# Attention and gated product: probabilities turned in float32 and split from PSUM, early exponentials per head, attention's buffers lent to later stages

## The chip, the cores and the metric

The kernel runs on one core of one Trainium2 chip. The metric is device time in microseconds (us) for one execution, lower is better. The engines are named as the profile names them: PE (TensorE, the matrix engine), PEld (its weight loads), DVE (VectorE), ACT (ScalarE), POOL (GpSimd) and SP, whose queue issues every DMA of this kernel.

## The reference, cut to what matters

```python
# q, k, v: [8, 8, 576, 64] (batch, head, row, depth); q and k are drawn 8 times larger than v
k_p = k.reshape(B, H, 72, 8, D).mean(axis=3)      # 8 rows pooled into one: 72 keys
v_p = v.reshape(B, H, 72, 8, D).mean(axis=3)
scores = (1 / 8) * q @ k_p.T
scores -= scores.max(-1)
attn = exp(scores); attn /= attn.sum(-1) + 1e-9
x = (attn @ v_p)  ->  [4608, 512]                 # 8 batches x 576 rows, 8 heads x 64
out = ((x @ w_a) * (x @ w_b)) @ w_out             # [512, 1536] twice, then [1536, 512]
```

Everything is float32, and the weights arrive as 8-byte words that the kernel itself converts.

## The kernel before, in words

**Precision.** A matmul operand is held as two rounded float32 parts (fp32r), a high part and a low part (the rest). A product is three matmuls: high by high, high by low, low by high. A "cast" to fp32r on ACT makes the high part, a subtraction (`low_part`) the low one.

**Attention.** The 4608 rows are 36 chunks of 128 rows (`chunk(i)`); a batch has 576 rows, so chunk 4 holds rows of two batches. Chunks 0 to 3 make the first tile of 512 rows (`early`). Per chunk: `qh`, `ql` are the parts of q; two PSUM banks `psc` take the scores of four heads each (72 columns per head); ACT copies them to `s` (all 8 heads, 576 columns); DVE takes the maximum `m`, subtracts it, ACT takes the exponential of all 576 columns, DVE takes the sum `z`, its reciprocal, and multiplies. The first 64 columns of each head then go to `pr`, as a high and a low part, and the last 8 columns to `rem`, which holds high, low and high again side by side. PE turns them (matmul with an identity, in transpose mode): four 128x128 blocks of the high part, four of the low part, two of `rem`, each set into a bank `ptr`, and ACT copies each bank out to `early_p` or `p` (the parts th, tl, tr). Two chunks make a block of 256 rows, whose products with the pooled values (`vdiag`, `vrem`) land in banks `po` and become x.

**The gated product.** x is handled in nine tiles of 512 rows. Tiles 0, 1 and 2 go through 12 column blocks f: `psa`, `psb` take x by w_a and w_b (weight buffers `jab`), DVE multiplies them into `h`, whose parts `hh`, `hl` are multiplied by w_out (`jo_open`, `jo_later`, `wo`) into four accumulator banks `acc`. The other six tiles are three pairs, (3,4), (5,6), (7,8), for which seven products of combinations of the two halves replace eight (banks `bank_psa`, `bank_psb`, `bank_att`, combinations `x_0` to `x_6`); the second tile of a pair keeps its gated values in device memory (`later`) and fetches them back (`back`) at the end of the pair. An accumulator that is finished is copied by ACT or DVE to a temporary `y` and stored (`give`).

**What sets the order.** Nothing in the kernel is a hand-written order on the engines: `Schedule.run` is a list planner that runs while the kernel is built. Each step is an `Op` with the engines it may run on and a cost per engine from the constants `FIXED`, `EACH` and `COLUMN`; generators (`chunk`, `ffn_in`, `both`, ...) yield steps and wait for marks, and the planner issues the step that can start first, by rank among the near ones. Every engine then runs its rows strictly in that order. So a change of one step's cost or engine moves rows on all engines. Buffers are handed out by name: eight PSUM banks (`banks`), and five SBUF temporaries of 512 columns, `tmps`, which serve `kp`, `vwide`, converted weight parts, `xo`, `back`, `gated` and `y`; `take(tmps)` blocks its generator until one is free.

**Weights at the start.** For each f, SP loads the 8-byte `words` of w_a, w_b (512 KB each) and w_out; ACT and DVE turn them into float32 (`wab`, `wo_first`), ACT and DVE or POOL split them into `jab` and `jo_open`. This runs between the rows of the first chunks.

In the profile every matmul has line L281, every turn L278, most ACT work L250, two-input DVE or POOL work L228, reductions L243.

Of the kernel before, what the change touches and what calls it, by code (L numbers as in the profile page):

```python
# [191 lines left out]
def attn_moe_kernel(ctx: ExitStack, tc: tile.TileContext, q, k, v, vr, wa, wb, wo, out):  # L192
# [49 lines left out]
    def red(out, in_, op):  # L242
        run = lambda e: nc.vector.tensor_reduce(out=out, in_=in_, axis=AX.X, op=op)  # L243
        return Op((SV,), run, [out], [in_], {SV: FIXED[SV] + EACH[SV] * size(in_)})
# [7 lines left out]
    def evict(out, in_):  # L252
        n = size(out)
        run = lambda e: nc.scalar.copy(out, in_) if e == SA else nc.vector.tensor_copy(out, in_)
# [460 lines left out]
    def load_keys(b):  # L715
# [6 lines left out]
        for g0 in range(0, NK, 2):  # L722
            gs = slice(g0, g0 + 2)
            for g in (g0, g0 + 1):
                if b == 0:
# [4 lines left out]
                yield red(kp[:, g, :], kraw.rearrange("p (s j) -> p s j", j=POOL), ALU.add)  # L730
                if b:
                    kv.append(kv_of["k", b, g])
            for e in range(2):
# [1 line left out]
                yield act(
                    kd[r, gs, 0, e, :], kp[r, gs],
                    lambda r=r, e=e: nc.scalar.mul(kd[r, gs, 0, e, :], kp[r, gs], 1.0 / POOL),  # L737
                )
# [59 lines left out]
    def chunk(i):  # L798
# [18 lines left out]
        yield W(("probs", i - 2))  # L817
        s = place(sb, [P, H, SP], F32, f"s{i % 2}", f"s_{i}")
        m = place(sb, [P, H], F32, f"m{i % 2}", f"m_{i}")
        z = place(sb, [P, H], F32, f"z{i % 2}", f"z_{i}")  # L820
        hk = 2 * SP
        for g0 in range(0, NK, 2):
            for b, lo, hi in flat[i]:
# [12 lines left out]
                yield copy(s[lo:hi, 2 * g0:2 * g0 + 4], pt[lo:hi, :2 * hk].rearrange("p (h s) -> p h s", h=4))  # L836
                banks.append(tag)
        mark("scores", i)
        yield red(m, s, ALU.max)
        yield tt(s, s, m.unsqueeze(2).broadcast_to([P, H, SP]), ALU.subtract)  # L840
        yield act(s, s, lambda: nc.scalar.activation(s, s, AF.Exp, scale=SCALE))
        yield red(z, s, ALU.add)
# [34 lines left out]
        for x in range(3):  # L877
            rows, num = (P, NK) if x < 2 else (NR, NG)
            dst = turned[j][x]
            srcs = [  # L880
                pr[:, x, 2 * g:2 * g + 2, :].rearrange("p a s -> p (a s)") if x < 2
                else rem[:, g].rearrange("p a c s -> p (a c s)")
                for g in range(num)
            ]
            yield until_ready(spare_time, *srcs)
            tag = yield from take(banks)
            pt = bank(tag, f"ptr_{i}_{x}")
            ptr = pt.bitcast(F32R).rearrange("p (g s) -> p g s", g=NK)
# [13 lines left out]
        th, tl, tr = (turned[j][x] for x in range(3))  # L902
# [297 lines left out]
    with tc.manual_schedule():  # L1200
        nc.vector.tensor_copy(ident, ident0)
        for t in kdiag + vdiag:
            nc.gpsimd.memset(t.bitcast(F32), 0.0)
        nc.vector.tensor_reduce(
            out=mask[:NR], in_=ident0[:NR, :NR].rearrange("p (a c s) -> p c a s", a=3, c=4), axis=AX.XY, op=ALU.add
# [81 lines left out]
```

## Time and profile before

| what | value |
|---|---|
| median of 3 runs (lowest, highest) | 1055.77 us (1054.13, 1060.22) |
| the profiled execution: its time, its span | 1054.74 us, 1052.6 us |
| PE busy, of the span | 1006.1 us (96%), 4896 matmuls |
| DVE, ACT, POOL busy | 640.0, 438.8, 212.7 us |
| DVE busy in the first 175 us, from the table of stretches below | 156.5 us |
| moved by DMA | 256.24 MB, 243 GB/s over the span |

The profiled execution's time is 1.03 us below the median of the runs. Between its span and its own time lie 2.1 us. The page's row for a matmul gives a modelled end, and matmuls follow each other before that end: a busy share of PE of 96% says when PE had work, not that it is at its peak. PE's clock as granted (PEclk) is 1.00 when full. All times in rows are us from the span's start unless marked ns; "x12" is a count of instructions.

### The profile page before, as it was taken

The numbers are of one execution on the slowest core, as the hardware profiler recorded it, in microseconds if no ns is written. First come the engines' busy times: TensorE is split into PE (matmuls) and PEld (weight loads), VectorE is DVE, ScalarE is ACT, GpSimd is POOL, SyncE is SP. The second block draws the span as 40 slices with busy tenths as digits, with TensorE's granted clock in tenths as the row PEclk, the third lists the DMA queues.
The fourth block names the chain that finished last, engine by engine and source line by source line (L and its number), as shares of the span: only waits on it lengthen the run. The fifth ranks groups of instructions, "written<-read, shape, count | busy, mean of one in ns | idle before, by whom it ended". The sixth has DMA issues, their size and how long they took to land.

```text
span 1052.6 us, 13699 instructions
## 1 busy us (share of the span) xinstructions
PE 1006.1 (96%) x4896; PEld 834.4 (79%) x4896; DVE 640.0 (61%) x978; ACT 438.8 (42%) x838; POOL 212.7 (20%) x164
## 2 busy tenths in 40 slices
PE   3698899999999999989999999999999999999998
PEld 3687688888888888868888887888888788888876
DVE  7998999988987556878775337333333633333321
ACT  5676666655565454554443314211111431111122
POOL 4221112011320001143121114022211501222100
PEclk9796999999999999989999999999999999999999
DMA  6494788789969989657765667666668966666792
GB/s 232 168 309 150 267 297 306 274 274 331 305 234 307 304 270 322 217 182 225 245 220 181 210 223 268 216 227 215 202 215 266 344 213 216 218 216 212 232 337 88
DMA packets 120467, 256.24 MB, mean 243 GB/s; under 512 B 10160, under 2 KB 26544, under 8 KB 120400
## 3 DMA queue, kind: packets, MB, share of 16 engines
q1 hardware_dynamic: 120400, 255.37, 73.0%
q8 instruction: 39, 0.64, 0.2%
q14 instruction: 28, 0.23, 0.1%
HBM read 195.82 MB, written 59.51 MB: 243 GB/s over the span
## 4 chain that ended last, share of the span: by engine, by line
PE 85%; DVE 6%; ACT 3%; DMA 3%; issue 1%; SPq 0%; POOL 0%; ACTq 0%; DVEq 0%; POOLq 0%
PE acc L281 26%; PE bank_psb L281 14%; PE bank_psa L281 9%; PE bank_att L281 9%; PE psb L281 8%; PE psa L281 8%; PE po L281 4%; PE psc L281 4%; PE ptr L278 2%; DMA words<-in_wo 1%; DMA vraw<-in_v 1%; DVE s L228 1%; ACT x L250 1%; DMA words<-in_wb 1%; DVE temp L228 1%
## 5 line engine op out<-in xcount | busy, mean ns | idle before, releaser
L281 PE MATMUL bank_psb<-x,j 128*128 128x512 f32 x648 | 167.7, 394 | 0.5 <-DVE temp L228 0.5
L281 PEld LDWEIGHTS bank_psb<-x,j 128*128 128x128 f32 x648 | 121.6, 189 | 27.4 <-DVE temp L228 1.1
L281 PE MATMUL acc<-jo_later,hh 128*128 128x512 f32 x384 | 124.2, 405 | 0.2
L281 PE MATMUL bank_psa<-x,j 128*128 128x512 f32 x432 | 111.5, 393 | 0.0
L281 PE MATMUL bank_att<-x,j 128*128 128x512 f32 x432 | 111.2, 392 | 0.0
L281 PE MATMUL psa<-xh,jab 128*128 128x512 f32 x288 | 102.5, 409 | 5.7 <-ACT jab L250 2.8
L281 PE MATMUL psb<-xh,jab 128*128 128x512 f32 x288 | 99.2, 397 | 0.5 <-DVE h L228 0.4
L228 DVE TENSOR_TENSOR temp<-bank_psb,temp 128x512 f32<-128x512 f32 x72 | 49.7, 690 | 78.4 <-PE bank_psb L281 77.2
L281 PEld LDWEIGHTS bank_psa<-x,j 128*128 128x128 f32 x432 | 81.0, 189 | 17.3
L281 PEld LDWEIGHTS bank_att<-x,j 128*128 128x128 f32 x432 | 80.3, 188 | 17.3 <-ACT temp L250 0.4
L228 DVE TENSOR_TENSOR temp<-bank_att,temp 128x512 f32<-128x512 f32 x54 | 37.3, 691 | 87.0 <-PE bank_att L281 81.1
L228 POOL TENSOR_TENSOR temp_p<-temp_p,temp 128x512 f32<-128x512 f32 x36 | 47.4, 1317 | 209.8 <-ACT temp_p L250 204.5
L228 DVE TENSOR_TENSOR temp<-bank_psa,temp 128x512 f32<-128x512 f32 x54 | 37.3, 691 | 81.2 <-PE bank_psa L281 77.4
L228 POOL TENSOR_TENSOR temp_h<-temp_h,temp 128x512 f32<-128x512 f32 x36 | 48.1, 1336 | 185.0 <-ACT temp_h L250 176.6
L228 POOL TENSOR_TENSOR ql<-qraw,qh 128x512 fp32r<-128x512 f32 x28 | 39.4, 1407 | 219.7 <-ACT qh L250 214.9
L281 PEld LDWEIGHTS acc<-jo_later,hh 128*128 128x128 f32 x384 | 68.5, 189 | 13.0 <-ACT hh L250 1.5
L281 PE MATMUL acc<-jo_later,hl 128*128 128x512 f32 x192 | 76.3, 398 | 0.0
L250 ACT CAST p<-ptr 128x512 fp32r<-128x512 f32 (+1 forms) x102 | 52.3, 514 | 48.1 <-PE ptr L278 47.9
L250 ACT CAST hh<-temp 128x512 fp32r<-128x512 f32 x36 | 22.4, 621 | 119.1 <-DVE temp L228 119.1
L281 PEld LDWEIGHTS psa<-xh,jab 128*128 128x128 f32 x288 | 55.7, 194 | 19.9 <-ACT jab L250 3.5
L281 PE MATMUL psc<-kdiag,qh 128*128 128x144 f32 x320 | 62.7, 292 | 7.6 <-ACT kdiag L737 7.0
L281 PEld LDWEIGHTS psc<-kdiag,qh 128*128 128x128 f32 x320 | 56.5, 210 | 11.2 <-issue 7.0
(137 smaller groups left out, 1967.6 us busy)
## 6 DMA issues: line engine op xcount, KB each, us to landing
j<-jd SPq DMA_DIRECT2D x108, 512.0 KB, 5.3
jo_later<-od SPq DMA_DIRECT2D x48, 512.0 KB, 3.8
wo<-od SPq DMA_DIRECT2D x36, 512.0 KB, 5.9
jab<-jd SPq DMA_DIRECT2D x34, 512.0 KB, 6.2
jd<-jab SPq DMA_DIRECT2D x24, 512.0 KB, 4.7
jd<-sums SPq DMA_DIRECT2D x24, 512.0 KB, 4.4
back<-later SPq DMA_DIRECT2D x43, 256.0 KB, 4.5
out<-y SPq DMA_DIRECT2D x36, 256.0 KB, 4.6
```

What stands on the lines that cost most here:

```text
L228: run = lambda e: vec[e].tensor_tensor(out=out, in0=in0, in1=in1, op=op)
L250: return act(out, in_, lambda: nc.scalar.copy(out, in_), rank)
L278: nc.tensor.transpose(to, lhs, rhs)
L281: nc.tensor.matmul(to, lhs, rhs, start=start, stop=stop, skip_group_check=bool(skip))
```

## The change

What it does, part by part:

- **Turn in float32.** The product with the reciprocal sum writes `pr` directly, as one float32 tile of 512 columns; the last 8 columns per head are multiplied apart (64 columns). PE turns `pr` in float32 with a float32 identity (`ident`; the fp32r one for `rem` is now `rounded`): one set of four blocks where there were two. The high part is cast by ACT out of the turned bank, the low part is the bank less the high part, on DVE. `rem`'s low part is pinned to DVE, and its two high copies are now split by group of heads.
- **Early exponentials per head.** For chunks below `BY_HEAD` = 8 whose rows are all of one batch (0 to 3, 5, 6, 7), DVE takes the negated maximum of four heads straight from the score bank, and ACT takes the exponential of each head from PSUM, with that maximum as its bias, writing `s` and, through its accumulator, the sum `z`. The copy to `s`, the subtraction, the long exponential and the sum over 576 columns are gone for these chunks. The factor 1/8 moves from the exponential into the keys.
- **Buffers.** `s`, `m`, `z` have three copies instead of two. Once all blocks are through the value product, `more_tmps` adds the five attention buffers `qh0`, `ql0`, `qh1`, `ql1`, `qraw` to `tmps`.
- **Rank.** `load_values(0)` gets a rank of -19.995.

```diff
+    def exponential(out, in_, bias, total):
+        run = lambda e: nc.scalar.activation(out, in_, AF.Exp, bias=bias, accum_out=total)
+        return Op((SA,), run, [out, total], [in_, bias], {SA: 0.36 + EACH[SA] * size(out)})
...
-                    lambda r=r, e=e: nc.scalar.mul(kd[r, gs, 0, e, :], kp[r, gs], 1.0 / POOL),
+                    lambda r=r, e=e: nc.scalar.mul(kd[r, gs, 0, e, :], kp[r, gs], SCALE / POOL),
...
+        direct = i < BY_HEAD and len(flat[i]) == 1
...
-                yield copy(s[lo:hi, 2 * g0:2 * g0 + 4], pt[lo:hi, :2 * hk].rearrange("p (h s) -> p h s", h=4))
+                if direct:
+                    yield red(m[:, hs4], four, ALU.max, True)
+                    for h in range(4):
+                        x = 2 * g0 + h
+                        yield exponential(s[:, x], four[:, h], m[:, x:x + 1], z[:, x:x + 1])
+                else:
+                    yield copy(s[lo:hi, hs4], four[lo:hi])
                 banks.append(tag)
...
-        yield tt(s, s, z.unsqueeze(2).broadcast_to([P, H, SP]), ALU.mult, (SG, SV))
         yield W(("turned", i - 2))
-        pr = place(sb, [P, 2, H, KM], F32R, f"pr{i % 2}", f"pr_{i}")
+        pr = place(sb, [P, H, KM], F32, f"pr{i % 2}", f"pr_{i}")
...
-        yield copy(pr[:, 0], s[:, :, :KM])
-        for x in (0, 2):
-            yield copy(rem[:, :, x], sr)
-        yield low_part(pr[:, 1], s[:, :, :KM], pr[:, 0], (SG, SV))
-        yield low_part(rem[:, :, 1], sr, rem[:, :, 0], (SG, SV))
+        yield tt(pr, s[:, :, :KM], spread(z, KM), ALU.mult, (SG, SV))
+        yield tt(sr, sr, spread(z, KR), ALU.mult)
+        for r in range(NG):
+            yield copy(rem[:, r, 0:3:2], sr[:, r].unsqueeze(1).broadcast_to([P, 2, 4, KR]))
+        yield low_part(rem[:, :, 1], sr, rem[:, :, 0])
...
-            yield pe([(ptr[:rows, g], srcs[g], ident) for g in range(num)], turn=True)
-            yield copy(dst[:rows, :, c0:c0 + P], ptr[:rows, :num])
+        yield pe([
+            (pt[:, g], pr[:, 2 * g:2 * g + 2].rearrange("p a s -> p (a s)"), ident) for g in range(NK)
+        ], turn=True)
+        yield copy(th[:, :, here], pt)
+        yield low_part(tl[:, :, here], pt, th[:, :, here])
...
+    def more_tmps():
+        yield W(*(("value", j) for j in range(block_of[-1] + 1)))
+        tmps.extend(["qh0", "ql0", "qh1", "ql1", "qraw"])
```

How rows move, at three places. First PE, chunks 2 and 3 of the first tile; `ptr_0`, `ptr_1`, `ptr_2` were the sets of the high part, the low part and `rem`, `psc_0_402` a score bank of chunk 4. Before:

```order
L278 MATMUL ptr_0_401<-ident,pr_357 128x128 x4
L281 MATMUL psc_0_402<-kdiag_77,qh_299 128x144 x2
L281 MATMUL psc_0_402<-kdiag_77,ql_300 128x144
L278 MATMUL ptr_1_418<-ident,pr_357 128x128 x4
L278 MATMUL ptr_2_424<-ident,rem_358 96x128 x2
L278 MATMUL ptr_0_459<-ident,pr_441 128x128 x4
L278 MATMUL ptr_1_466<-ident,pr_441 128x128 x4
L278 MATMUL ptr_2_473<-ident,rem_442 96x128 x2
```

The same two chunks in the changed kernel, PE:

```order
L284 MATMUL ptr_385<-ident,pr_357 128x128 x4
L284 MATMUL ptr_rem<-rounded,rem_358 96x128 x2
L284 MATMUL ptr_429<-ident,pr_417 128x128 x4
L284 MATMUL ptr_rem<-rounded,rem_418 96x128 x2
L287 MATMUL po_0_451<-p_1_380,vdiag_79 128x256
```

One set of four is gone per chunk, and the score matmuls of chunk 4 are no longer among the turns but behind the first `psa` rows.

Second, DVE in chunk 0, from the scores to the turn (`vp` is a pooled value, `wab_75` holds raw values there). Before:

```order
L243 TENSOR_REDUCE m_144<-s_143 128x8
L228 TENSOR_TENSOR s_143<-s_143,m_144 128x576
L243 TENSOR_REDUCE m_168<-s_167 128x8
L243 TENSOR_REDUCE z_145<-s_143 128x8
L843 TENSOR_SCALAR z_145<-z_145 128x8
L844 RECIPROCAL z_145<-z_145 128x8
L228 TENSOR_TENSOR s_143<-s_143,z_145 128x576
L243 TENSOR_REDUCE vp_183<-wab_75 96x64 x2
L235 SCALAR_TENSOR_TENSOR vwide_243<-vp_183,mask 96x256 x2
L228 TENSOR_TENSOR pr_230<-s_143,pr_230 128x512
```

The changed kernel, DVE, from its second maximum of chunk 0:

```order
L245 TENSOR_REDUCE m_171<-psc_0_176 128x4
L245 TENSOR_REDUCE m_144<-psc_2_192 128x4
L864 TENSOR_SCALAR z_145<-z_145 128x8
L865 RECIPROCAL z_145<-z_145 128x8
L230 TENSOR_TENSOR pr_219<-s_143,z_145 128x512
L230 TENSOR_TENSOR s_143<-s_143,z_145 128x8x8
L245 TENSOR_REDUCE vp_186<-wab_75 96x64
L230 TENSOR_TENSOR rem_220<-s_143,rem_220 128x2x32
L245 TENSOR_REDUCE vp_186<-wab_75 96x64
L230 TENSOR_TENSOR early_p_83<-ptr_250,early_p_83 128x4x128
```

The rows over 576 columns are gone; the low part (`early_p_83` from `ptr_250`) now stands behind the turn instead of ahead of it.

Third, ACT at the end of the second pair, where four accumulators are copied out to `y` while the combinations `x_0`, `x_4`, `x_3` of the next pair are cast. Before:

```order
L254 COPY y_0_7458<-acc_0_6653 128x512
L254 COPY y_1_7464<-acc_1_6666 128x512
L254 COPY y_2_7470<-acc_2_6691 128x512
L250 CAST hh_7476<-back_7441 128x512
L250 CAST x_0_7478<-x_7349 128x1024
L250 CAST jo_later<-back_7454 128x512
L250 CAST x_4_7482<-temp_2_7486 128x1024
L250 CAST x_3_7481<-temp_2_7485 128x1024
L254 COPY y_3_7497<-acc_3_6711 128x512
```

The changed kernel, ACT, same place:

```order
L256 COPY y_0_7266<-acc_0_6461 128x512
L256 COPY y_1_7272<-acc_1_6474 128x512
L256 COPY y_2_7277<-acc_2_6499 128x512
L256 COPY y_3_7283<-acc_3_6519 128x512
L252 CAST hh_7285<-back_7247 128x512
L252 CAST jo_later<-back_7254 128x512
```

The fourth copy moved from behind five casts to right behind the third.

More of the change, by code (lines that the diff above doesn't have):

```diff
@@ L39 @@
 LAG = 5
+BY_HEAD = 8
+VALUES_0 = -19.995
 JOIN, STEP = 40, 8
@@ L240, in ts, with red @@
         return Op((SV,), run, [out], [in0], {SV: FIXED[SV] + 0.0005 * size(out)})
-    def red(out, in_, op):
-        run = lambda e: nc.vector.tensor_reduce(out=out, in_=in_, axis=AX.X, op=op)
+    def red(out, in_, op, negate=False):
+        run = lambda e: nc.vector.tensor_reduce(out=out, in_=in_, axis=AX.X, op=op, negate=negate or None)
         return Op((SV,), run, [out], [in_], {SV: FIXED[SV] + EACH[SV] * size(in_)})
@@ L290, in tmp @@
         return place(sb, [P, 512], dtype, tag, name)
-    ident0 = tmp(tmps[0], "ident0")[:, :P]
-    make_identity(nc, ident0)
-    ident = const.tile([P, P], F32R, name="ident")
+    ident = const.tile([P, P], F32, name="ident")
+    make_identity(nc, ident)
+    rounded = const.tile([P, P], F32R, name="rounded")
     def big(tag, name):
@@ L741, in load_keys @@
                 yield stt(
-                    kd[r, gs, 1, e, :], kp[r, gs], 1.0 / POOL, kd[r, gs, 0, e, :].bitcast(F32), ALU.mult, ALU.subtract
+                    kd[r, gs, 1, e, :], kp[r, gs], SCALE / POOL, kd[r, gs, 0, e, :].bitcast(F32), ALU.mult, ALU.subtract
                 )
@@ L816, in chunk, with spread @@
             qs.append(tag)
[L817 to L820, printed above, removed]
+        yield W(("probs", i - 3))
+        s = place(sb, [P, H, SP], F32, f"s{i % 3}", f"s_{i}")
+        m = place(sb, [P, H], F32, f"m{i % 3}", f"m_{i}")
+        z = place(sb, [P, H], F32, f"z{i % 3}", f"z_{i}")
         hk = 2 * SP
+        direct = i < BY_HEAD and len(flat[i]) == 1
+        def spread(x, n):
+            return x.unsqueeze(2).broadcast_to([P, H, n])
         for g0 in range(0, NK, 2):
@@ L835, in chunk @@
                 ])
-                yield copy(s[lo:hi, 2 * g0:2 * g0 + 4], pt[lo:hi, :2 * hk].rearrange("p (h s) -> p h s", h=4))
-                banks.append(tag)
[L838 to L842, printed above, removed]
+                if g0 == NK - 2 and hi == P:
+                    mark("scores", i)
@@ new lines, in chunk @@
+                hs4 = slice(2 * g0, 2 * g0 + 4)
+                four = pt[:, :2 * hk].rearrange("p (h s) -> p h s", h=4)
+                if direct:
[5 more added lines that the diff above has]
+                    yield copy(s[lo:hi, hs4], four[lo:hi])
+                banks.append(tag)
@@ L843, in chunk @@
+        if not direct:
+            yield red(m, s, ALU.max)
+            yield tt(s, s, spread(m, SP), ALU.subtract)
+            yield act(s, s, lambda: nc.scalar.activation(s, s, AF.Exp))
+            yield red(z, s, ALU.add)
         yield Op((SV,), lambda e: nc.vector.tensor_scalar_add(z, z, 1e-9), [z], [z], {SV: 0.17})
         yield Op((SV,), lambda e: nc.vector.reciprocal(z, z), [z], [z], {SV: 0.2})
-        yield tt(s, s, z.unsqueeze(2).broadcast_to([P, H, SP]), ALU.mult, (SG, SV))
         yield W(("turned", i - 2))
-        pr = place(sb, [P, 2, H, KM], F32R, f"pr{i % 2}", f"pr_{i}")
+        pr = place(sb, [P, H, KM], F32, f"pr{i % 2}", f"pr_{i}")
@@ L876, in chunk @@
                 turned[j].update({y: three[:, y * NK:y * NK + (NK if y < 2 else NG)] for y in range(3)})
[L877 to L888, printed above, removed]
-            yield pe([(ptr[:rows, g], srcs[g], ident) for g in range(num)], turn=True)
-            yield copy(dst[:rows, :, c0:c0 + P], ptr[:rows, :num])
-            banks.append(tag)
+        th, tl, tr = (turned[j][x] for x in range(3))
+        here = slice(c0, c0 + P)
+        yield until_ready(spare_time, pr)
+        tag = yield from take(banks)
+        pt = bank(tag, f"ptr_{i}").rearrange("p (g s) -> p g s", g=NK)
+        yield pe([
[3 more added lines that the diff above has]
+        yield low_part(tl[:, :, here], pt, th[:, :, here])
+        banks.append(tag)
+        yield until_ready(spare_time, rem)
+        tag = yield from take(banks)
+        pt = bank(tag, f"ptr_{i}_rem").bitcast(F32R).rearrange("p (g s) -> p g s", g=NK)
+        yield pe([
+            (pt[:NR, r], rem[:, r].rearrange("p a c s -> p (a c s)"), rounded) for r in range(NG)
+        ], turn=True)
+        yield copy(tr[:NR, :, here], pt[:NR, :NG])
+        banks.append(tag)
         mark("turned", i)
@@ L901, in chunk @@
         cols = slice(j * BLOCK - t * NT, j * BLOCK - t * NT + BLOCK)
-        th, tl, tr = (turned[j][x] for x in range(3))
         for g0 in range(0, NK, 2):
@@ L1200, in attn_moe_kernel @@
     with tc.manual_schedule():
-        nc.vector.tensor_copy(ident, ident0)
+        nc.vector.tensor_copy(rounded, ident)
         for t in kdiag + vdiag:
@@ L1204, in attn_moe_kernel @@
         nc.vector.tensor_reduce(
-            out=mask[:NR], in_=ident0[:NR, :NR].rearrange("p (a c s) -> p c a s", a=3, c=4), axis=AX.XY, op=ALU.add
+            out=mask[:NR], in_=ident[:NR, :NR].rearrange("p (a c s) -> p c a s", a=3, c=4), axis=AX.XY, op=ALU.add
         )
```

6 lines of the change are left out of this document (4 added, 2 removed).

## Prediction, made before the run

> **What bounds the kernel now.** I read the page's table of engines, then a table of stretches, PE's waits, and last the rows around single waits.
>
> ```profile
> PE 1006.1 (96%) x4896; PEld 834.4 (79%) x4896; DVE 640.0 (61%) x978; ACT 438.8 (42%) x838; POOL 212.7 (20%) x164
> ```
>
> That alone says "PE". The stretches (columns: stretch and length, then busy us and count of PE, PEld, DVE, ACT, POOL, granted clock, DMA share, GB/s) say where it is not:
>
> ```profile
> 0.00:27.00 27.00, 9.92 (x46) 9.28 (x46) 21.32 (x35) 15.46 (x32) 12.08 (x22) 1.00 0.68 228
> 27.00:53.00 26.00, 17.79 (x86) 16.39 (x87) 23.83 (x35) 17.30 (x36) 6.96 (x4) 0.76 0.50 173
> 53.00:79.00 26.00, 25.70 (x131) 21.58 (x130) 23.84 (x37) 19.07 (x37) 7.52 (x6) 0.98 0.92 308
> 79.00:105.00 26.00, 21.63 (x105) 18.62 (x106) 21.25 (x34) 16.04 (x35) 4.38 (x3) 0.67 0.46 148
> 105.00:130.00 25.00, 22.04 (x113) 17.22 (x113) 22.89 (x33) 18.11 (x32) 4.58 (x3) 1.00 0.81 275
> 130.00:175.00 45.00, 44.17 (x220) 35.91 (x219) 43.37 (x67) 29.27 (x56) 8.44 (x5) 1.00 0.88 296
> 175.00:452.00 277.00, 277.00 (x1514) 234.77 (x1513) 215.90 (x351) 158.83 (x317) 39.22 (x28) 1.00 0.85 282
> 452.00:458.00 6.00, 2.08 (x11) 1.41 (x9) 5.84 (x8) 5.89 (x9) 1.72 (x2) 0.90 0.80 279
> 458.00:1052.60 594.60, 585.74 (x2680) 479.18 (x2680) 261.74 (x387) 158.87 (x290) 127.82 (x92) 0.99 0.68 225
> ```
>
> Three regimes. Up to 105 us PE idles 17.1 + 8.2 + 0.3 + 4.4 = 30 us, and its clock falls to 0.76 and 0.67, while DVE is busy 90.24 of 105 us: the start is paced by DVE and by the chain through one chunk. From 175 to 452 PE has no gap, so there only fewer or shorter PE rows help. After that it loses 3.9 us in one place (452 to 458) and 8.9 us in a few more. PE's waits name them:
>
> ```profile
> PE ptr L278 <- ACT pr L250: 17.5, 4, 6.1
> PE psc L281 <- ACT kdiag L737: 7.0, 1, 7.0
> PE ptr L278 <- ACT s L250: 4.3, 2, 3.9
> PE acc L281 <- ACT y L254: 2.2, 1, 2.2
> PE acc L281 <- DVE y L254: 1.8, 1, 1.8
> ```
>
> The turns waited 17.5 us for `pr`, all at the start; 3.9 us is the gap at 453 us; the two waits for `y` lie at the pairs' ends.
>
> **Term 1, one set of turns fewer per chunk.** PE's rows in the dense part (start, duration, then x2 or x4 instructions):
>
> ```profile
> 360.24 0.62 PE L281 MATMUL psb<-xh,jab 128*128 128x512 f32 x2
> 360.70 0.40 PE L281 MATMUL psb<-xl,jab 128*128 128x512 f32 x1
> ...
> 361.17 0.46 PE L278 MATMUL ptr<-ident,pr 128*128 128x128 f32 x4
> 361.47 0.70 PE L281 MATMUL acc<-jo_later,hh 128*128 128x512 f32 x2
> 362.01 0.39 PE L281 MATMUL acc<-jo_later,hl 128*128 128x512 f32 x1
> ```
>
> Start to start a set of four takes 0.30 us, and the two matmuls behind it 0.54 where two take 0.46 elsewhere: 0.38 us, or less where a score matmul follows; I take 0.36. The trace counts the sets from 175 us on:
>
> ```profile
> L278 PE MATMUL ptr<-ident,pr x208: 222/244/370, 204.5 to 600.0; 128*128 128x128 f32 x104
> ```
>
> 208 are 52 sets, half of them low parts: 26 x 0.36 = 9.4 us, all on the path. The ten earlier chunks' sets fall where PE waits anyway: 0.
>
> This holds if a float32 turn costs what an fp32r turn costs. No float32 matmul is in the trace. From below, the row above (0.30 us a set), and I exclude a gain, since words of the same width are loaded and streamed. From above, four passes: each turn as four streams of 128 columns, which is one row of 512 columns, 0.23 us, so 0.92 us a set, or, with the weights loaded four times too, 4 x 0.30 = 1.20. I take the row: the turn already runs on 4-byte words, and a turn only moves them.
> The Trainium skill, "FP8 and Floating Point Precision", TensorE Precision Notes, says that true FP32 takes four passes through the array; by that alone the 36 sets would cost up to 36 x 0.9 = 32 us more. The same skill, "TensorE: Matmul & The Clock Gate", Terms (row xbus), says of trn2's transpose mode that it is 4x faster for FP32, which would cancel it. No row here shows either.
>
> **Term 2, DVE in the early chunks.** Groups of DVE and ACT in 0 to 175 us (busy us, mean ns | idle before), and among them one row of the timeline (start, duration), of 64 columns on DVE:
>
> ```profile
> L228 DVE TENSOR_TENSOR s<-s,m 128x576 f32<-128x576 f32 x10 | 11.5, 1154 | 0.4
> L228 DVE TENSOR_TENSOR s<-s,z 128x576 f32<-128x576 f32 x10 | 8.3, 834 | 0.3
> L243 DVE TENSOR_REDUCE m<-s 128x8 f32<-128x576 f32 x11 | 8.2, 743 | 1.5 <-ACT s L250 1.5
> L243 DVE TENSOR_REDUCE z<-s 128x8 f32<-128x576 f32 x10 | 7.4, 745 | 0.7 <-ACT s L841 0.5
> L228 DVE TENSOR_TENSOR pr<-s,pr 128x512 fp32r<-128x512 f32 x8 | 6.6, 820 | 0.0
> 29.85 0.21 DVE L228 TENSOR_TENSOR rem<-s,rem 128x64 fp32r<-128x64 f32 x1
> L228 DVE TENSOR_TENSOR xl<-po,xh 128x512 fp32r<-128x512 f32 x8 | 5.5, 686 | 6.3 <-ACT xh L250 6.3
> L250 ACT COPY s<-psc 128x288 f32<-128x288 f32 x21 | 8.2, 399 | 5.2 <-PE psc L281 3.4 <-DVE rem L228 1.6
> L841 ACT ACTIVATE s<-s 128x576 f32<-128x576 f32 x10 | 6.9, 687 | 3.2 <-DVE s L228 3.1
> L250 ACT CAST pr<-s 128x512 fp32r<-128x512 f32 x10 | 6.2, 620 | 6.1 <-DVE s L228 6.0
> L250 ACT CAST p<-ptr 128x512 fp32r<-128x512 f32 x16 | 9.4, 586 | 5.4 <-PE ptr L278 5.4
> L250 ACT CAST rem<-s 128x64 fp32r<-128x64 f32 x20 | 4.0, 242 | 0.0
> ```
>
> A direct chunk loses on DVE 1.154 + 0.834 + 0.743 + 0.745 + 0.820 = 4.30 us. It gains two maxima over 288 columns from PSUM (between 0.2 and 0.74 each; I take half of the 576-column row, 0.37), the product into `pr` (0.82, the same shape), the small product (0.21, the 64-column row) and the low part from PSUM (0.69, by the row xl<-po,xh): 2 x 0.37 + 0.82 + 0.21 + 0.69 = 2.46. That saves 1.8 us per chunk, 12.9 over seven. An ordinary chunk exchanges 0.83 + 0.82 for 0.82 + 0.21 + 0.69: 0.1 more, over 29 chunks 2 us, under a DVE that in 175 to 452 is busy 78%: 0.
>
> What reaches PE: the first four chunks' 7 us, since up to 105 us PE waits for what DVE makes; the other three chunks' saving comes where PE lacks little (3.8 us in 105 to 175) and I count 0. So -7, bounds 0 and -17 (12.9, and half the time lost at clock 0.67 in 79 to 105, 26 x 0.33 / 2 = 4).
>
> **ACT** gets eight exponentials of 72 columns for two copies, one long exponential, the cast of `pr` and the cast of the turned low part: out 0.80 + 0.69 + 0.62 + 0.59 = 2.70 us per chunk. One of 72 columns with bias and accumulator is in no row; 0.24 (the 64-column cast) and 0.69 (the 576-column exponential) are its ends. I take 0.35, near the short one: 2.8 us, no change. At 0.69 it is 5.5, so 2.8 x 4 = 11 us more in the first 53, where ACT is busy 32.8: still under 53, but the chain through a chunk would be as long as before and term 2 would be 0.
> The Trainium skill, "ScalarE: Activation LUTs", What ACT_TABLE_LOAD costs, gives about 280 ns + 0.833 ns a column for an ACTIVATE with a pointer bias, so 0.34 us, an estimate without the accumulator; the sum would be the same.
>
> POOL's multiplies only change names; the pinned `rem` part is the 64-column row. On SP's queue the second pair of `kraw` loads now stands ahead of the second `words`, which also wait for a conversion that moved back on DVE. Their slack:
>
> ```profile
> 25.75 0.33 SPq L261 DMA_DIRECT2D words<-in_wa  x1
> ...
> 38.54 1.13 ACT L463 ACTIVATE wab<-words 128x1024 f32<-128x1024 f32 x1
> words<-in_wa SPq DMA_DIRECT2D x12, 512.0 KB, 4.7
> ```
>
> They were asked for at 25.8 us and first read at 38.5, 12.8 later; the last row, of the DMA issues, has 4.7 us to landing. So 8 us of cover; 0, and if it is gone, the second weight block is late next.
>
> **Term 3, more temporaries.** At the pairs' ends ACT's fourth `y` stood behind casts because, as the order and `take(tmps)` read, no temporary was free; now it stands right behind the third. That removes the 2.2 and 1.8 us waits. The clock there:
>
> ```profile
> 644.00:650.00 6.00, 4.16 (x15) 3.00 (x14) 6.00 (x8) 5.13 (x6) 2.57 (x3) 0.83 0.98 356
> ```
>
> 6 x 0.17 = 1 us of clock was lost too; I count half: -4.5, bounds 0 (the next PE row then waits for `back`, with DMA at 0.98) and -5.
>
> **Term 4, start of the pairs.** The gap at 453 us is a turn that waits for a bank behind ACT's casts of `x`. Now score and `rem` rows of about 1.1 us stand ahead of the second product, which needs those casts as well. -1, bounds -4 and +3.
>
> **Sum.** -9.4 - 7 - 4.5 - 1 = -21.9 us on 1054.74, so 1032.8; the median of the runs is 1.03 above its profiled run: 1034 us.
>
> **Rivals.**
> (a) Only the turns pay. For it: in 53 to 79 DMA is at 0.92, so the weights' loads could bind what DVE leaves, and a freed wait often moves on. Against it: in 0 to 53 DMA is at 0.68 and 0.50. Then -9.4 to -12: 1045.
> (b) The start pays more: all seven chunks' DVE time and the clock, -17 for term 2: 1024.
> (c) Slower: float32 turns run in four passes with four loads. In the dense part 26 sets cost 0.9 us more, +23.4, in the start 10 more sets up to +9, against -21.9 of the rest: 1057 to 1066, say 1061. It decides from 0.84 us more per set, at 1.14 us a set; at 0.92 the 26 sets give +16, so still about 1050. For it: no float32 turn was ever timed here. Against it: the rows of the fp32r turns show plain 4-byte words.
> (d) The change does not do what it says: the planner's rows are placed by its constants, and new waits eat the rest (low parts of turned banks hold `ptr` until DVE gets there, which is busy 43.37 of 45 us in 130 to 175): 1051 to 1056.
>
> **How the numbers follow.** My forecast 0.52, (a) 0.21, (b) 0.14, (c) 0.07, (d) 0.06. About 0.5% (5.3 us) is what a measurement of this kernel can tell from no change: under 1050.5 lie the forecast, (a) and (b), 0.87; (d) and a part of (c) are within it, 0.08; slower is most of (c), 0.05. The range 1021 to 1050 holds the forecast, most of (b) and (a); the forecast's own is 1027 to 1040.
>
> **What would show it.** PE's turns of `pr`: 144 rows of 128x128, median still about 245 ns (four passes would show 0.4 us or more, or sets over 0.9 us start to start). Exponentials: 56 rows near 0.35 us. PE idle before 105 us near 23 instead of 30, the first `psa` matmul some 4 us ahead of its row:
>
> ```profile
> 50.44 0.79 PE L281 MATMUL psa<-xh,jab 128*128 128x512 f32 x1 [0.50 <-DVE xl L228]
> ```
>
> No waits of `acc` for `y` in the middle. PE without gaps in about 170 to 440, shorter by 9 us. I am wrong if turned sets are longer, if PE waits for `words` or `p` low parts, or if the gaps at the pairs' ends come back with another name.

## The result, and the profile after

The changed kernel takes 1027.86 us (median of 4 runs, 1026.47 to 1030.40) against 1056.46 (1054.13 to 1060.22) for the kernel before on the same chip: ratio 0.9729, 95% interval 0.9692 to 0.9765. The forecast was 1034.0, with a range of 1021 to 1050. The profiled execution took 1026.70 us, its span is 1024.7; before they were 1054.74 and 1052.6.

The engines' line and the table of stretches after (columns as in the prediction):

```profile
PE 985.5 (96%) x4752; PEld 821.4 (80%) x4752; DVE 626.2 (61%) x1007; ACT 410.0 (40%) x859; POOL 210.9 (21%) x162
```

```profile
0.00:27.00 27.00, 13.45 (x56) 11.95 (x57) 21.54 (x43) 18.08 (x74) 11.47 (x21) 1.00 0.68 230
27.00:53.00 26.00, 20.89 (x99) 18.38 (x99) 23.09 (x40) 21.18 (x52) 6.04 (x4) 0.80 0.69 237
53.00:79.00 26.00, 16.97 (x64) 12.84 (x63) 24.09 (x41) 15.28 (x41) 6.57 (x5) 0.67 0.82 283
79.00:105.00 26.00, 26.00 (x146) 22.20 (x146) 19.93 (x37) 20.13 (x60) 4.18 (x4) 1.00 0.65 219
105.00:130.00 25.00, 24.85 (x129) 20.52 (x128) 23.69 (x36) 17.30 (x32) 4.88 (x4) 1.00 0.75 257
130.00:175.00 45.00, 45.00 (x243) 38.45 (x242) 40.27 (x61) 28.57 (x54) 7.95 (x5) 1.00 0.88 297
175.00:424.00 249.00, 249.00 (x1280) 209.95 (x1279) 188.32 (x319) 121.80 (x244) 33.66 (x22) 1.00 0.87 289
424.00:445.00 21.00, 15.91 (x79) 13.07 (x78) 15.85 (x25) 11.56 (x17) 8.14 (x5) 0.84 0.50 163
445.00:1024.70 579.70, 573.46 (x2669) 474.00 (x2667) 269.37 (x414) 156.05 (x291) 128.03 (x95) 1.00 0.70 234
```

The regimes are the same, but the start's bad stretch (PE idle for 9.0 us, clock 0.67) now stands at 53 to 79 us instead of 79 to 105, and after it PE hardly stops until 424 us; before, 3 us were still missing in 105 to 130. The gap at the start of the pairs is larger: 5.1 us idle in 424 to 445, against 3.9 in 452 to 458 before. PE's waits:

```profile
PE psc L287 <- ACT kdiag L743: 7.9, 1, 7.9
PE ptr L284 <- DVE s L230: 7.3, 3, 3.3
PE ptr L284 <- DVE pr L230: 5.4, 1, 5.4
PE ptr_rem L284 <- ACT s L252: 2.7, 1, 2.7
PE psc L287 <- DVE p L230: 2.7, 2, 1.9
```

The turns' 17.5 us of waiting for `pr` have become 7.3 + 5.4, and `acc` no longer waits for `y` at all.

**A ledger of PE.** Stretches of equal length hold different work, so I count work instead. Each matmul gets its own start-to-start time where rows stand dense, a median of the two traces: 0.2275 us for 512 columns, 0.1125 for 256, 0.1115 for 144; a set of turns with what it costs the two rows behind it 0.44 (four in float32), 0.368 (four in fp32r), 0.19 (two of `rem`). "Lost" at a point is the time there less the work issued so far: what PE lost to gaps, to low clock and to rows slower than the dense ones. All matmuls are in both traces. Cumulative, in us:

| kernel | work in all | lost at first `psa` | at 109th `psa` (about 150 us) | at last `acc` of tile 2 | at first `bank_att` | at first row of pair 2 | of pair 3 | at last `acc` |
|---|---|---|---|---|---|---|---|---|
| before | 965.2 | 37.1 | 55.7 | 60.4 | 67.1 | 74.9 | 80.1 | 83.0 |
| after | 954.6 | 31.1 | 48.7 | 50.9 | 59.7 | 63.3 | 63.8 | 65.4 |

The 28.2 us between the two last `acc` rows are 10.65 of work and 17.5 of loss: 7.0 up to the 109th `psa`, 2.5 more up to the end of tile 2, then 2.1 back at the start of the pairs, and 10.1 in the pairs, of which 4.3 + 3.1 at the ends of the first two (cut finer than the table: between a pair's last `bank_att` of its products and the next pair's first row).

### The profile page after: what moved, and what is told of

Same layout as the page of the kernel before. It is cut to its first block, busy times and chain, and to the rows that moved or that the text cites. A ratio compares the mean times of both kernels' runs of the same rounds, so it can differ in the third digit from the quotient of the medians.

```text
span 1024.7 us, 13483 instructions
## 1 busy us (share of the span) xinstructions
PE 985.5 (96%) x4752; PEld 821.4 (80%) x4752; DVE 626.2 (61%) x1007; ACT 410.0 (40%) x859; POOL 210.9 (21%) x162
## 4 chain that ended last, share of the span: by engine, by line
PE 85%; DVE 5%; DMA 5%; ACT 2%; issue 1%; POOL 1%; SPq 0%; ACTq 0%; DVEq 0%; POOLq 0%
PE acc L287 28%; PE bank_psb L287 13%; PE bank_att L287 9%; PE bank_psa L287 9%; PE psb L287 9%; PE psa L287 9%; PE po L287 4%; PE psc L287 4%; DMA vraw<-in_v 1%; PE ptr L284 1%; DMA j<-jd 1%; DMA qraw<-in_q 1%; DVE temp L230 1%; DMA wo_rest<-in_v 1%; DMA kraw<-in_k 1%
## 5 line engine op out<-in xcount | busy, mean ns | idle before, releaser
L287 PE MATMUL acc<-jo_later,hh 128*128 128x512 f32 x384 | 121.6, 398 | 0.3
L287 PE MATMUL psa<-xh,jab 128*128 128x512 f32 x288 | 99.9, 400 | 0.1
L287 PE MATMUL psc<-kdiag,qh 128*128 128x144 f32 x320 | 61.8, 289 | 13.3 <-ACT kdiag L743 7.9
L287 PE MATMUL acc<-jo_open,hh 128*128 128x512 f32 x192 | 62.8, 409 | 0.8 <-ACT s L260 0.7
```

The lines of the kernel that those rows point to most:

```text
L287: nc.tensor.matmul(to, lhs, rhs, start=start, stop=stop, skip_group_check=bool(skip))
```

## The experiments

Each kernel is timed against the kernel before on its own chip, whose medians were 1059.3 (the first four kernels), 1057.0 (the next four) and 1059.7 us (the last four); so the ratios are compared, and "scaled" is the ratio times 1056.46. Differences between two ratios are uncertain by about 5 us. The ledger of each profiled execution, columns as above:

| kernel | ratio, 95% | scaled | work | first `psa` | 109th `psa` | tile 2 | first `bank_att` | pair 2 | pair 3 | end |
|---|---|---|---|---|---|---|---|---|---|---|
| after | 0.9729 (0.9692 to 0.9765) | 1027.8 | 954.6 | 31.1 | 48.7 | 50.9 | 59.7 | 63.3 | 63.8 | 65.4 |
| e1 | 0.9907 (0.9884 to 0.9930) | 1046.6 | 954.6 | 33.2 | 55.7 | 59.9 | 69.2 | 77.2 | 82.3 | 85.6 |
| e2 | 0.9862 (0.9821 to 0.9903) | 1041.9 | 954.6 | 33.8 | 64.7 | 70.2 | 76.7 | 80.5 | 80.9 | 83.3 |
| e3 | 0.9774 (0.9744 to 0.9805) | 1032.6 | 954.6 | 31.1 | 50.2 | 52.4 | 64.3 | 73.6 | 78.3 | 79.5 |
| e4 | 0.9835 (0.9816 to 0.9854) | 1039.0 | 970.4 | 32.1 | 48.8 | 50.8 | 60.6 | 63.1 | 63.6 | 65.3 |
| e5 | 0.9815 (0.9791 to 0.9838) | 1036.9 | 954.6 | 33.7 | 58.6 | 61.8 | 67.8 | 71.2 | 73.8 | 77.8 |
| e6 | 0.9816 (0.9790 to 0.9841) | 1037.0 | 954.6 | 31.5 | 57.2 | 63.5 | 70.2 | 76.7 | 77.2 | 79.7 |
| e7 | 0.9823 (0.9798 to 0.9847) | 1037.8 | 954.6 | 30.8 | 57.6 | 61.3 | 71.8 | 75.9 | 76.4 | 78.2 |
| e8 | 0.9859 (0.9841 to 0.9878) | 1041.6 | 954.6 | 31.9 | 50.1 | 54.2 | 76.3 | 79.1 | 79.6 | 81.0 |
| e9 | 0.9778 (0.9752 to 0.9804) | 1033.0 | 954.6 | 37.2 | 55.3 | 57.3 | 67.1 | 70.4 | 70.8 | 73.2 |
| e10 | 0.9872 (0.9847 to 0.9896) | 1042.9 | 954.6 | 41.0 | 64.2 | 66.2 | 75.0 | 78.9 | 79.4 | 81.0 |
| e11 | 0.9948 (0.9929 to 0.9967) | 1051.0 | 965.2 | 34.6 | 56.9 | 60.7 | 64.8 | 71.7 | 78.5 | 81.6 |
| e12 | 0.9697 (0.9666 to 0.9728) | 1024.4 | 954.6 | 31.9 | 52.6 | 55.5 | 61.3 | 64.2 | 64.7 | 69.1 |

Theory A was that the parts of the change add up by the ledger; the main rival was that the planner's new order makes the time.

**e1, the turn alone.** Against the changed kernel:

```diff
-BY_HEAD = 8
+BY_HEAD = 0
-        yield W(("probs", i - 3))          # and s, m, z in two copies
+        yield W(("probs", i - 2))
-        ... need(b) - 1.0 if b else VALUES_0)
+        ... need(b) - 1.0)
-        sch.spawn(more_tmps(), 0.0)
```

> Only the turn in float32 is kept (with the split from the bank); no chunk takes its exponentials per head, the buffers of s and the temporaries are those of before. Theory A (a ledger of parts): in the changed kernel's trace a set of four float32 turns takes 0.355 us and 0.085 us in the two matmuls behind it, 0.44; before, two sets took 2 x (0.295 + 0.073) = 0.74. So 36 x 0.296 = 10.7 us less, nearly all on the path, and the start stays: first psa row at about 49 us (before 50.4), time about 1046. Rival B (the start's gain comes from the turn: one bank, one PE set and one cast less between the probabilities and the first value product): first psa at 43 to 45 us, time 1038 to 1040. Rival C (the planner's new order makes the time, no part does): anywhere from 1040 to 1060, and the gaps in places that neither trace has.

Measured: 9.8 us faster than before by the ratio, about the 10.65 us of work. The first `psa` came 5.1 us earlier than before (the row below against 50.44), close to rival B's 43 to 45 and not theory A's 49. But nothing of that lead lasted: at the 109th `psa` the loss is 55.7, as before.

```profile
45.29 0.54 PE L287 MATMUL psa<-xh,jab 128*128 128x512 f32 x1
```

So the first `psa` is a poor measure of the start, and the turn alone came out at about its work. Its order of rows is neither that of before nor that of the changed kernel, so this agreement may be partly luck (see e7).

**e2, no exponentials per head.**

```diff
-BY_HEAD = 8
+BY_HEAD = 0
```

> The changed kernel with the early exponentials per head undone (no chunk takes them), all else kept. Theory A: the start goes back: first psa at 49 to 50 us instead of 42.6, time lost by PE to gaps and low clock up to about 150 us back from 48.7 to about 55 us, total about 1028 + 7 = 1035. Rival B (the turn made the start shorter): first psa stays at 43 to 45, total 1028 to 1030. Rival C (the planner's order): no fixed relation, 1025 to 1040, with the start's gaps elsewhere.

Measured: 14.1 us back by the ratio, twice what theory A said, and the ledger puts 16.0 of it before the 109th `psa`. But the first `psa` was only 3.4 us later than in the changed kernel (45.99 us); most was lost behind it, where PE now waited for weights as well (`jab`, no such wait in the changed kernel):

```profile
PE psa L287 <- DVE jab L230: 3.5, 3, 1.7
PE psa L287 <- ACT jab L252: 3.1, 2, 2.1
```

e2 changes the planner's order everywhere, so it doesn't price the exponentials alone; e9 was made for that.

**e3, without the lent buffers.**

```diff
-        sch.spawn(more_tmps(), 0.0)
```

> The changed kernel without the five attention buffers added to the temporaries; all rows up to about 600 us stay in the same order on every engine. Theory A: the two long waits of acc for y come back at the ends of the first two pairs, and with them the lower clock behind them: PE lost 5.0 us at the first and 3.8 us at the second before, 0.7 and 0.7 after, so about +7.4: 1035. Rival B (the waits move: the pairs' ends then wait for the second tile's stored values or for loads): +0 to +3, 1028 to 1031. Rival C (the gain at the pairs' ends comes from the order of the casts alone, not from the buffers): 1028, no acc-for-y waits.

Measured: 4.8 us back by the ratio (7.5 by the medians, which come from two chips), between theory A and the upper end of rival B. Both waits are back, so rival C falls:

```profile
PE acc L287 <- DVE y L256: 3.1, 1, 3.1
PE acc L287 <- ACT y L256: 2.5, 2, 2.3
```

In the ledger of its profiled execution, the slowest of its four, the ends of the first two pairs lose 7.0 and 5.0 us, against 0.7 and 0.7 with the buffers. Another 3 us of this execution were lost at the start of the pairs, where the order is the same as in the changed kernel (last section).

**e4, every float32 set twice**, in the order of the changed kernel.

```diff
-            for to, lhs, rhs, *more in calls:
+            for to, lhs, rhs, *more in calls * (2 if turn and calls[0][2] is ident else 1):
```

> Every float32 set of four turns is issued twice into the same bank, the second overwriting the first; the order of rows on all engines is that of the changed kernel. Theory A (a float32 turn costs PE one stream of the block and is on the path): each extra set costs 4 x 0.089 = 0.36 us; 36 sets are 12.8 us if all lie on the path (1041), 9.3 if only the 26 of the dense part do (1037). Rival D (four passes): an extra set costs 0.92 to 1.2 us, +24 to +43 us (1052 to 1071). Rows: a set of eight takes about 0.71 us start to start, against 1.3 or more.

Measured: 11.2 us more by the ratio, 15.7 between the profiled executions. A set of eight takes 0.79 us, so the second four cost 0.435, not 0.36:

```profile
315.92 1.03 PE L284 MATMUL ptr<-ident,pr 128*128 128x128 f32 x8
316.71 0.43 PE L287 MATMUL psc<-kdiag,qh 128*128 128x144 f32 x2
```

That is 36 x 0.435 = 15.7 us of work, and the loss stayed what it was (65.3 against 65.4 at the end, 48.8 against 48.7 at the 109th `psa`). So the sets of the start were on the path like those of the dense part, by the ledger; the ratio alone could not tell 36 sets from 26. Rival D is excluded.

**e5, two copies of s and the rank undone.**

```diff
-        yield W(("probs", i - 3))          # and s, m, z in three copies
+        yield W(("probs", i - 2))
-        ... need(b) - 1.0 if b else VALUES_0)
+        ... need(b) - 1.0)
```

> The changed kernel with s, m, z in two copies again and the rank of the first values undone; exponentials per head, float32 turn and the lent buffers kept. It tells what undoing the exponentials alone measured (+16.5 us): Theory A (the exponentials make the start, copies and rank are small): 1028 to 1031, first psa at 42 to 44 us, time lost by PE up to 150 us near 49. Rival E (copies or rank make half of it, the exponentials only use them): lost time up to 150 us back at about 55, total 1034 to 1038.

Measured: 9.1 us slower than the changed kernel, rival E's size. The loss up to the 109th `psa` is 58.6, more than before the change.

**e6, only the first four chunks.**

```diff
-BY_HEAD = 8
+BY_HEAD = 4
```

> Only the first tile's four chunks take their exponentials per head; chunks 5, 6 and 7 go the ordinary way. The prediction counted the first four alone. Theory A1 (first four alone): 1028 to 1031. Rival F (the three chunks between 45 and 130 us count as much, because DVE is what the first weights and PE wait for there): first psa stays at 42 to 43 us, but PE's lost time from first psa to 150 us grows from 17.5 by some 5 to 9 us: 1033 to 1037.

Measured: 9.2 us slower, 8.5 of it up to the 109th `psa`, all behind the first `psa`. That is rival F's size, but e7 makes it doubtful as a proof.

**e7, only the planner's price of an exponential.**

```diff
-        return Op((SA,), run, [out, total], [in_, bias], {SA: 0.36 + EACH[SA] * size(out)})
+        return Op((SA,), run, [out, total], [in_, bias], {SA: 0.47 + EACH[SA] * size(out)})
```

> The planner's fixed price of an exponential per head is 0.47 instead of 0.36 us, which makes it 0.53 with its 72 columns, what the trace shows with the accumulator read (325 + 208 ns). Theory A: rows move only in the first 130 us; the turn of chunk 4, which now waits 5.4 us for the probabilities at 59 us, stands later on PE: up to 5 us faster, 1023 to 1028. Rival C (the planner's order is a lottery within a few us): 1026 to 1034, with a gap of the same kind elsewhere.

Measured: 9.9 us slower, beyond what either theory allowed, though the same operations are issued and the price is nearer to the truth. Not only their order differs: the planner also moved a few to another engine (in all 14 rows more on DVE and 13 fewer on POOL). The stretch from 45 to 105 us, first of the changed kernel, then of e7, and three of e7's rows with waits in it; the first has a counterpart of 5.38 us in the changed kernel, the other two have none:

```profile
45.00:105.00 60.00, 50.97 (x253) 41.96 (x253) 50.80 (x88) 41.17 (x112) 13.05 (x10) 0.86 0.77 267
```

```profile
45.00:105.00 60.00, 44.63 (x206) 35.77 (x205) 52.86 (x89) 40.36 (x107) 9.92 (x6) 0.76 0.77 258
```

```profile
68.03 1.11 PE L284 MATMUL ptr<-ident,pr 128*128 128x128 f32 x4 [6.27 <-DVE pr L230]
...
81.06 1.09 PE L284 MATMUL ptr<-ident,pr 128*128 128x128 f32 x4 [1.16 <-DVE s L230]
84.68 0.45 PE L284 MATMUL ptr_rem<-rounded,rem 128*96 128x128 f32 x2 [2.53 <-DVE p L230]
```

PE is idle for 6.3 us more and its clock is lower for longer. So the plan alone (the order of rows and the engine of a few) moves this kernel by 10 us, 8.9 of it in the ledger up to the 109th `psa`, as much as the parts under study; e1, e2, e5, e6 and e8 hold such a share too, and none of them can be read as the price of its edit.

**e8, exponentials per head in all chunks of one batch.**

```diff
-BY_HEAD = 8
+BY_HEAD = 36
```

> Every chunk of one batch (32 of 36) takes its exponentials per head. Per chunk it takes about 1.8 us from DVE and gives ACT 8 x 0.53 for 2.7 us, +1.5. Theory A (in the dense part neither engine is on the path): PE's lost time from 175 us on stays at about 16 us, total 1028, within 3. Rival G (DVE's relief shortens the start of the pairs and the bank holds): 1023 to 1025. Rival H (ACT's 200-ns accumulator reads delay the casts that PE waits for at the start of the pairs): 1031 to 1035.

Measured: 13.7 us slower, outside all three ranges. Up to the end of tile 2 it loses 3.3 us more than the changed kernel, and then 22 at the start of the pairs against 8.8, most of it around one wait of 13.2 us:

```profile
441.60 3.42 DVE L230 TENSOR_TENSOR x<-x,temp 128x512 f32<-128x512 f32 x2
...
444.95 2.35 DVE L230 TENSOR_TENSOR x<-temp,x 128x512 fp32r<-128x512 f32 x2
...
447.22 2.48 DVE L230 TENSOR_TENSOR x<-x,x 128x512 fp32r<-128x512 f32 x4
449.63 0.16 DVE L864 TENSOR_SCALAR z<-z 128x8 f32<-128x8 f32 x1
...
450.06 0.69 DVE L230 TENSOR_TENSOR pr<-s,z 128x512 f32<-128x512 f32 x1
...
452.80 0.45 DVE L245 TENSOR_REDUCE m<-psc 128x4 f32<-128x288 f32 x1
...
454.53 0.20 ACT L260 ACTIVATION_READ_ACCUMULATOR s<-psc,m 128x1 f32 x1
...
454.78 1.12 PE L284 MATMUL ptr<-ident,pr 128*128 128x128 f32 x4 [13.18 <-ACT s L260]
```

A turn stood on PE in front of the pair's first product. Its probabilities `pr` stood on DVE behind 8 us of combinations `x` and were ready at 450.75. But the turn started 4 us later, and what it waited for last is ACT's `s`: four exponentials of another chunk, which end at 454.73 and whose maximum `m` stood still further back in DVE's queue. They write nothing that the turn reads, so what they set free is most likely its bank; the trace does not name banks. Rival H had the place and, for the last 1.3 us, the engine (four exponentials with their accumulator reads); most of the wait is DVE's queue, which it did not name.

**e9, DVE's time given back**, in the order of the changed kernel; `twice` issues an op's instruction two times at the planner's price of one.

```diff
-                    yield red(m[:, hs4], four, ALU.max, True)
+                    yield twice(red(m[:, hs4], four, ALU.max, True))
...
-        yield tt(pr, s[:, :, :KM], spread(z, KM), ALU.mult, (SG, SV))
+        op = tt(pr, s[:, :, :KM], spread(z, KM), ALU.mult, (SG, SV))
+        yield twice(op) if direct else op
```

> The order of rows on every engine is that of the changed kernel; in the seven chunks with exponentials per head the two maxima and the product into pr are issued twice, 2 x 0.45 + 0.77 = 1.67 us of DVE per chunk, about what the change had taken away, 6.7 us in the first four chunks and 11.7 in all seven. Theory A (what DVE is spared shortens the start, as term 2 had it): first psa 4 to 7 us later than 42.6, PE's lost time up to 150 us from 48.7 to 55 or more, total 1035 to 1040. Rival C (the start is made by where the planner puts the rows; the DVE time itself is covered): first psa within 2 us, total 1028 to 1031.

Measured: 5.2 us slower by the ratio, 7.8 between the profiled spans (1032.5 and 1024.7). The first `psa` is 6.1 us later for 6.7 us of DVE in the first four chunks, and 6.6 us are lost more at the 109th `psa`; DVE's work in chunks 5 to 7 (5 us) adds about 0.5.

```profile
48.67 0.69 PE L287 MATMUL psa<-xh,jab 128*128 128x512 f32 x1
```

With the order held, theory A's mechanism shows: up to the first `psa`, nearly all of DVE's added time is PE's time. The total, 1033.0 scaled, is a little under its 1035 to 1040. The added rows stand both in DVE's queue and in the chain of steps through each chunk; e9 does not tell which of the two passes them on.

**e10, ACT's exponentials twice**, in the order of the changed kernel.

```diff
-                        yield exponential(s[:, x], four[:, h], m[:, x:x + 1], z[:, x:x + 1])
+                        yield twice(exponential(s[:, x], four[:, h], m[:, x:x + 1], z[:, x:x + 1]))
```

> Same order of rows; each exponential per head, with its accumulator read, is issued twice, 8 x 0.53 = 4.3 us of ACT more per chunk, 17 us in the first four and 30 in all seven. If ACT's price is on the path of the start (the bound of the prediction: at 0.69 us each the gain of term 2 is gone): first psa 8 to 17 us later, total 1036 to 1048. If ACT has cover there (it is busy 18 + 21 of the first 53 us): first psa at most 3 us later, total 1028 to 1032.

Measured: 15.1 us slower by the ratio, 15.6 between the spans; the first `psa` at 52.42 us is 9.8 later for 17 us of ACT, and all is lost by the 109th `psa` (64.2 against 48.7). So ACT's exponentials are not covered in the start: each us added to them costs PE about 0.6 up to the first `psa`.

**e11, the kernel before with the rank only.**

```diff
-            ... need(b) - 4.0 if b > 1 else need(b) - 1.0)
+            ... need(b) - 4.0 if b > 1 else need(b) - 1.0 if b else -19.995)
```

> The kernel before with nothing but the rank of the first values changed (-19.995), so that only the planner's order differs. Rival C (the order alone moves such a kernel by several us): 1045 to 1068, at least 4 us away from 1057 in the stretch from 7 to 150 us. Theory A (the order matters little without the other parts): 1055 to 1059. Faster than 1050 would mean that this rank makes a good part of the start's gain by itself.

Measured: 5.5 us faster by the ratio (3.5 to 7.5), scaled 1051. It moved, as rival C says, but the ledger up to 150 us moved by 1.2 in the other direction: not the place I named. In this trace the rank by itself makes no part of the start's gain.

**e12, chunk 4 planned later.**

```diff
-        spare_time = MARGIN if i >= early else 0.0
+        spare_time = (4.0 if i == early else MARGIN) if i >= early else 0.0
```

> The changed kernel with chunk 4's steps on PE planned 2.5 us later (margin 4.0 instead of 1.5), because its turn stands 5.4 us in front of its probabilities at 59 us and a spell of half clock follows. Theory A (that wait and its clock can be bought back by placing the turn later): 1021 to 1026, the wait of ptr for pr below 3 us. Rival C (any change of the plan in that stretch gives another wait, and the changed kernel's order is a good draw): 1030 to 1040.

Measured: the lowest ratio of all, 1024.4 scaled, but its interval overlaps that of the changed kernel: not told apart. Theory A's time came without its mechanism, since the wait for `pr` is not below 3 us:

```profile
PE ptr L284 <- DVE pr L230: 6.6, 1, 6.6
```

and the profiled execution lost 3.9 us more up to the 109th `psa` than the changed kernel. Rival C's times fail as well. I claim no improvement.

## Why the prediction was right, and where its steps were off

The measured 1027.9 us lies 6 us below the forecast of 1034, inside its own 1027 to 1040 but at the edge. The turns, the start and the temporaries paid, as forecast; the sizes of the single steps came out less well than their sum:

| step | predicted | by the ledger |
|---|---|---|
| 1, turns | -9.4 | -10.65 |
| 2, start | -7 | -7.0 |
| 3, more temporaries | -4.5 | -7.4 |
| 4, start of the pairs | -1 | +2.1 |
| not in the sum | 0 | -5.2 |
| sum | -21.9 | -28.2 |

**Term 1: near in sum by luck, from two errors of opposite sign.** "A float32 turn costs what an fp32r turn costs" failed by a little: a row's median is 272 ns, not 245. The 144 rows, and a set in the dense part with the row behind it:

```profile
L284 PE MATMUL ptr<-ident,pr x144: 270/272/473, 16.4 to 589.2; 128*128 128x128 f32 x144
```

```profile
357.32 0.60 PE L284 MATMUL ptr<-ident,pr 128*128 128x128 f32 x4
357.68 0.48 PE L287 MATMUL psb<-xh,jab 128*128 128x512 f32 x1
```

The set takes 0.36 us start to start, against 0.30 in fp32r, and the matmul behind it 0.31 us to the next one, where a matmul of 512 columns otherwise takes 0.23. Counted like that, two fp32r sets cost 2 x 0.368 us a chunk and one float32 set now costs 0.44: 0.296 saved, not 0.36. "The ten earlier chunks' sets: 0" failed as well; e4 shows the sets of the start on the path. 36 x 0.296 = 10.65. Rival (c) asked for 0.92 us or more a set.
The Trainium skill, "FP8 and Floating Point Precision", TensorE Precision Notes, has four passes for true FP32: four streams of 128 columns would be 0.23 us a turn, an estimate, and e4's extra turns took 0.109. So its rule does not hold for these turns. The 4x of "TensorE: Matmul & The Clock Gate", Terms (row xbus), for FP32 in transpose mode is the nearer rule, but it does not bring them down to the 0.06 to 0.09 us of the fp32r turns either (last section).

**Term 2: right in size, in part by luck; e9 bears out the mechanism; a price inside was wrong.** DVE's rows came as forecast (low part 683 ns against 686) or a little dearer (maxima 451 ns against 370). The exponential did not: "near 0.35 us" holds for the ACTIVATE only, and its accumulator is a second instruction.

```profile
L260 ACT ACTIVATE s<-psc,m 128x72 f32<-128x72 f32 x56 | 17.4, 325 | 2.9 <-DVE m L245 2.7
L260 ACT ACTIVATION_READ_ACCUMULATOR s<-psc,m 128x1 f32 x56 | 11.6, 208 | 0.0
L245 DVE TENSOR_REDUCE m<-psc 128x4 f32<-128x288 f32 x14 | 6.2, 451 | 2.6 <-PE psc L287 2.6
L230 DVE TENSOR_TENSOR p<-ptr,p 128x512 fp32r<-128x512 f32 x8 | 5.5, 683 | 1.1 <-ACT p L252 1.1
```

0.53 us, in all 56 x 0.18 = 10 us of ACT more than I wrote, of which, by e10, about half reaches PE. "No change" for ACT was therefore wrong, and the start gained 7 us in spite of it: something else there must have given as much back. It is not shown what; the plan alone can be worth 10 us (e7). "The first four alone" is left open: e6 speaks against it, e9 for it (chunks 5 to 7 added about 0.5 us), and e6 has another order.

The signs that I named were chosen badly: the first `psa` came 7.9 us ahead and not 4, PE idled 27.7 us before 105 us (from the stretches) and not 23, since the kernel was by then further in its work; and e1 shows a lead at that row that is worth nothing. Two signs of being wrong did appear, longer sets and waits for low parts `p` (2.7 us with `psc`, above), and neither cost as much as the change gained.

```profile
42.58 0.69 PE L287 MATMUL psa<-xh,jab 128*128 128x512 f32 x1
```

**Term 3: right mechanism, too small a size.** The stretches around the first two pairs' ends, before and then after:

```profile
640.00:660.00 20.00, 18.16 (x70) 14.05 (x70) 18.24 (x21) 12.08 (x17) 9.70 (x6) 0.91 0.79 280
825.00:845.00 20.00, 17.69 (x75) 13.50 (x74) 18.62 (x22) 13.35 (x19) 12.77 (x6) 1.00 0.91 326
```

```profile
617.00:637.00 20.00, 19.90 (x87) 15.78 (x86) 16.04 (x17) 13.19 (x19) 13.43 (x9) 1.00 0.81 291
795.00:815.00 20.00, 19.90 (x87) 15.76 (x86) 13.96 (x16) 11.92 (x18) 10.82 (x8) 1.00 0.95 332
```

The idle time before was 1.84 + 2.31 and the clock cost 20 x 0.09 = 1.8 more, all of which is gone: 5.8 of the ledger's 7.4 us. I had counted half of 1 us of clock, and set the bound at -5, which the ledger's 7.4 passes. e3 puts the term at 4.8 by the ratio and 10.6 in the ledger of its slowest execution, so its size is known only roughly.

**Term 4: wrong sign, inside its bounds.** At 424 us PE's next rows need a bank whose low part stands on DVE behind the combinations, and then `rem`'s turn waits for a copy to `s` that stands on ACT behind casts of `x`:

```profile
425.87 0.68 DVE L230 TENSOR_TENSOR p<-ptr,p 128x512 fp32r<-128x512 f32 x1
...
426.70 0.42 PE L287 MATMUL psc<-kdiag,qh 128*128 128x144 f32 x2 [1.90 <-DVE p L230]
...
433.17 0.33 PE L284 MATMUL ptr_rem<-rounded,rem 128*96 128x128 f32 x2 [2.73 <-ACT s L252]
```

That is rival (d)'s mechanism, "low parts of turned banks hold `ptr`", at one place and for 2 us. I had looked at what was moved there, and not at what the low part's new place behind the turn costs in a queue full of `x`.

**What the sum did not have.** 5.2 us: 1.9 between the 109th `psa` and tile 2, 0.6 to its end, 2.7 in the rest of the pairs. No experiment isolates them; a gain from the order is likely but not shown. The 1.9 lie where I had called PE free of gaps because its busy share was 100%: a busy PE still lost 2.7 us there.

Of the rivals, (a) and (c) are out; (b) named a total near the measured one, but by a start of -17, and the start gave 7.

## What to carry to other kernels

Count PE's work by start-to-start times and compare the time lost at equal work: it separates what an edit removes from what the order gives or takes, where stretches of equal length do not. Where a planner sets the order, an edit undone is no price of the edit: hold the order and issue the suspected instruction twice, and run a kernel or two that change the plan alone, to know the scatter (here 5.5 and 9.9 us). And count an activation's accumulator as an instruction of its own before it goes on the path.

## What the runs showed of the hardware

**Low clock comes in steps.** Summed over 1-us stretches, the time lost to a clock below 1.00 (1 less the granted clock, times the length) is near a multiple of 1.7 us in every trace I summed: in 50 to 175 us 8.5 in the changed kernel, 6.8 in e9, 10.2 in e10, 13.7 in e7, always at a clock of 0.50, so in spells of 3.4 us. The Trainium skill, "TensorE: Matmul & The Clock Gate", What's actually happening, states a free-running window of about 3.4 us and half rate; these runs agree with the two figures, and do not show when a window starts. Since, by that section, the window is not tied to the kernel, the same order can lose a different number of them. In 430 to 470 us, where PE has the same order in both, first the changed kernel, then e3:

```profile
430.00:470.00 40.00, 36.81 (x193) 31.11 (x192) 30.63 (x55) 15.95 (x36) 11.91 (x9) 0.95 0.57 183
```

```profile
430.00:470.00 40.00, 36.93 (x169) 30.78 (x169) 28.85 (x51) 16.34 (x34) 12.16 (x9) 0.85 0.54 174
```

The idle time is the same (3.2 and 3.1 us), but low clock takes 40 x 0.15 = 6 us in e3 and 40 x 0.05 = 2 in the changed kernel; the ledger has 3.1 of these 4 us as PE's loss up to the first `bank_att`. About 3 us of waiting thus came once with 2 and once with 6 us of low clock, and a difference of that size between two single profiles is no finding.

**A float32 turn** of 128 columns took 0.109 us from one to the next inside a set (e4 and the changed kernel), an fp32r one 0.060, 0.065 and 0.087 us (medians of the three steps inside a set of four, before).
